# A decode step with cached attention: K turned as 32-bit words, P turned on VectorE, scores and PV in four column tiles

## The chip, the core and the metric

The kernel runs on one core of a Trainium2 chip. The metric is device time in microseconds (us), from launch to end, as the median of several runs. "Span" is the stretch that the profile covers, from the first to the last instruction of one execution; for the kernel before it is 121.3 us where the time is 123.2 us.

## What is computed

Eight tokens (B = 8, one position each) of width 512 go through layer normalisation, then through two branches: attention over a cached window, and a feed-forward net (FFN) with a gelu gate. The window W is 1024 of the 4096 cached positions; there are 32 query heads on 8 K/V heads, head width 128.

```
def reference(A_x, A_k_cache, A_v_cache, A_wq, A_wo, B_x, B_w_gate, B_w_up, B_w_down):
    xn = _layernorm(A_x)
    q = (xn @ A_wq).reshape(8, 1, 32, 128).transpose(0, 2, 1, 3)
    k = jnp.repeat(A_k_cache[:, :, 4096 - 1024:, :], 4, axis=1)
    v = jnp.repeat(A_v_cache[:, :, 4096 - 1024:, :], 4, axis=1)
    p = softmax(einsum("bhqd,bhkd->bhqk", q, k) * 128 ** -0.5)
    s = einsum("bhqk,bhkd->bhqd", p, v).transpose(0, 2, 1, 3).reshape(8, 1, 4096) @ A_wo
    g = silu((gelu(xn @ B_w_gate) * (xn @ B_w_up)) @ B_w_down)
    return A_x + s * g
```

All inputs are bf16. The K and V windows are 16 MB each, wq and wo 4 MB each, and the three FFN weights 1.75 MB each: some 47 MB that are read once.

## The kernel before

**Loads.** Every large operand goes through one ring of 20 slots of 8 KB per partition, 1 MB each (`slot`, line 73), all issued on the sync queue in program order: K of group 0, four pieces of wq, K of group 1, and then, in the main loop (line 428), V of group g and K of group g + 2, and after these the FFN weights and wo in pieces (`parts`, line 439). A piece waits for the slot that it takes to be free, and for the transfer eight places before it on the queue.

**Groups.** A group is one token and one half of the K/V heads: 4 heads of 1024 positions, 16 groups in all. The slot of a group holds in each of its 128 partitions 32 rows (`NKR`) of 128 bf16, partition 4p + n having head n. So each 128x128 block of a K slot mixes the four heads, partition by partition. Scores are computed for all 16 queries of a group (`QW`: 4 heads by 4 queries) against every key, and those of the wrong head are pushed to minus 30000 by a mask that a small matmul adds (`hot` by `far`, line 242).

**Work of a group, before.** `turn_k` (226): 32 bf16 transposes on TensorE, eight to a PSUM tile, and one VectorE copy (234) for each eight. `score` (237): the mask matmul, and 32 matmuls with a turned K block as the loaded operand and the 16 queries as the streaming one (253). Scores come out with the keys in the partitions. `soft` (264): one exponential on ScalarE (266). `values` (269): a matmul with all ones that sums P over partitions (273), 32 matmuls with a V block loaded and P streaming (282), and on VectorE a reduction of the sums (290), a reciprocal (293) and the product (294). The output of a group is already turned, as wo needs it. `regroup` (301) packs eight tokens' outputs into `og`.

**Order.** The program order on each engine is the order of the code: nothing is moved by a scheduler (`manual_schedule`). In the main loop turning and scoring of group g alternate by eights, and `values` of group g - 1 comes before the last quarter of the scores of g:

Of the kernel before, what the change touches and what calls it, by code (L numbers as in the profile page):

```python
# [8 lines left out]
ACT = mybir.ActivationFunctionType  # L9
# [7 lines left out]
def kernel(  # L17
# [13 lines left out]
    nc = tc.nc  # L31
# [28 lines left out]
    kT_pool = ctx.enter_context(tc.tile_pool(name="kT_pool", bufs=8))  # L60
    p_pool = ctx.enter_context(tc.tile_pool(name="p_pool", bufs=3))
    small = ctx.enter_context(tc.tile_pool(name="small", bufs=3))
    ffn_sb = ctx.enter_context(tc.tile_pool(name="ffn_sb", bufs=1))
    ps_t = ctx.enter_context(tc.tile_pool(name="ps_t", bufs=2, space=bass.MemoryType.PSUM))
    ps_sc = ctx.enter_context(tc.tile_pool(name="ps_sc", bufs=2, space=bass.MemoryType.PSUM))
# [39 lines left out]
    def load_down(h):  # L105
        t = slot()
        n = FR // 2 * D
        nc.sync.dma_start(
            out=t[:, 0:n],
            in_=B_w_down.rearrange("(p j) d -> p (j d)", j=FR)[:, h * n : (h + 1) * n],  # L110
        )
        return t
# [3 lines left out]
    def load_wo(h0, j0, j1):  # L116

        t = slot()
        n = (j1 - j0) // rep if j1 - j0 > rep else 1
        if n > 1:  # L120
            nc.sync.dma_start(
                out=t[:, 0 : n * rep * D].rearrange("p (h f) -> p h f", h=n),
                in_=wo_rows[:, h0 : h0 + n, :],
            )
        else:
            nc.sync.dma_start(
                out=t[:, 0 : (j1 - j0) * D],
                in_=wo_rows[:, h0, j0 * D : j1 * D],
            )
        return t  # L130
# [7 lines left out]
    for g in range(NGR):  # L138
        v_t[g] = None
    stream = []  # L140
# [13 lines left out]
    ones_pp = consts.tile([P, P], BF16, name="ones_pp")  # L154
    nc.vector.memset(ones_pp, 1.0)
# [3 lines left out]
    hot = consts.tile([HN, P], BF16, name="hot")  # L159
    nc.vector.memset(hot, 0.0)  # L160
    nc.gpsimd.affine_select(
        out=hot.rearrange("n (p m) -> n p m", m=HN),
        in_=hot.rearrange("n (p m) -> n p m", m=HN),
# [3 lines left out]
        pattern=[[0, P // HN], [-1, HN]],  # L167
        channel_multiplier=1,
    )
    far = consts.tile([HN, NKR, QW], BF16, name="far")  # L170
    nc.vector.memset(far, -30000.0)
    nc.gpsimd.affine_select(
        out=far.rearrange("n r (m j) -> n r m j", m=HN),
        in_=far.rearrange("n r (m j) -> n r m j", m=HN),
# [3 lines left out]
        pattern=[[0, NKR], [-1, HN], [0, rep]],  # L178
        channel_multiplier=1,
    )  # L180
# [19 lines left out]
    for t in range(2):  # L200
        nc.scalar.dma_start(
            out=x_res[64 * t : 64 * t + B, :], in_=x_flat[:, t * 256 : (t + 1) * 256]
        )
    xT_ps = ps_t.tile([P, 2, NDC, 32], BF16, name="t_ps")
# [13 lines left out]
    qT_all = persist.tile([P, NHALF, B, HN, rep], BF16, name="qT_all")  # L218
    oT_all = persist.tile([P, NHALF, HN, rep, B], BF16, name="oT_all")
    og = persist.tile([P, Hkv, rep, 64], BF16, name="og")  # L220
    nc.vector.memset(og, 0.0)

    kT_t = {}
    sc_t = {}

    def turn_k(g, t):
        kp = ps_t.tile([P, 8 * P], BF16, name="t_ps")
        for c in range(8):
            r = 8 * t + c
            nc.tensor.transpose(  # L230
                kp[:, c * P : (c + 1) * P], k_t[g][:, r * Dh : (r + 1) * Dh], ident
            )
        kT = kT_pool.tile([P, 8 * P], BF16, name="kT")
        nc.vector.tensor_copy(out=kT, in_=kp)  # L234
        kT_t[g, t] = kT

    def score(g, t):
        b, i = groups[g]
        if t == 0:
            sc = ps_sc.tile([P, NKR, QW], FP32, name="sc_ps")  # L240
            sc_t[g] = sc
            nc.tensor.matmul(  # L242
                sc.rearrange("p r q -> p (r q)"),
                hot,
                far.rearrange("n r q -> n (r q)"),
                start=True,
                stop=False,
                skip_group_check=True,
            )
        sc = sc_t[g]  # L250
        for c in range(8):
            r = 8 * t + c
            nc.tensor.matmul(  # L253
                sc[:, r, :],
                kT_t[g, t][:, c * P : (c + 1) * P],
                qT_all[:, i, b, :, :].rearrange("p n j -> p (n j)"),
                start=False,
                stop=True,
                skip_group_check=True,
            )  # L260

    p_t = {}

    def soft(g):
        p = p_pool.tile([P, NKR, QW], BF16, name="p")
        nc.scalar.activation(out=p, in_=sc_t[g], func=ACT.Exp, scale=inv_sqrt_dh)  # L266
        p_t[g] = p

    def values(g):
        b, i = groups[g]  # L270
        p = p_t[g]
        sums_ps = ps_a.tile([P, NKR, QW], FP32, name="a_ps")
        nc.tensor.matmul(  # L273
            sums_ps.rearrange("p r q -> p (r q)"),
            ones_pp,
            p.rearrange("p r q -> p (r q)"),
            start=True,
            stop=True,
        )
        o_ps = ps_o.tile([P, QW], FP32, name="o_ps")  # L280
        for r in range(NKR):
            nc.tensor.matmul(  # L282
                o_ps,
                v_t[g][:, r * Dh : (r + 1) * Dh],
                p[:, r, :],
                start=(r == 0),
                stop=(r == NKR - 1),
            )
        sums = small.tile([P, QW], FP32, name="sums")
        nc.vector.tensor_reduce(  # L290
            out=sums, in_=sums_ps.rearrange("p r q -> p q r"), axis=AX.X, op=ALU.add
        )
        nc.vector.reciprocal(out=sums, in_=sums)  # L293
        nc.vector.tensor_tensor(  # L294
            out=oT_all[:, i, :, :, b],
            in0=o_ps.rearrange("p (n j) -> p n j", n=HN),
            in1=sums.rearrange("p (n j) -> p n j", n=HN),
            op=ALU.mult,
        )

    def regroup(i):

        rg = ps_a.tile([P, rep, HN, B], FP32, name="a_ps")
        sel = ident.rearrange("p (e j) -> p j e", j=rep)
        for j in range(rep):
            for c in range(rep):
                nc.tensor.matmul(
                    rg[32 * c : 32 * c + 32, j, :, :],
                    sel[:, j, :],
                    oT_all[:, i, :, c, :],  # L310
                    start=True,
                    stop=True,
                    skip_group_check=True,
                    tile_position=(0, 32 * c),
                )
        nc.vector.tensor_copy(
            out=og[:, i * HN : (i + 1) * HN, :, 0:B],
            in_=rg.rearrange("p j h b -> p h j b"),
        )
# [19 lines left out]
    q_sb = persist.tile([P, NHALF, 512], BF16, name="q_sb")  # L339
    nc.vector.tensor_copy(out=q_sb[:, 0, :], in_=q_ps[0])  # L340
    nc.scalar.copy(out=q_sb[:, 1, :], in_=q_ps[1])
    for i in range(NHALF):
        qT_ps = ps_t.tile([P, rep, HN, 32], BF16, name="t_ps")
        for c in range(rep):
            nc.tensor.transpose(  # L345
                qT_ps[:, c, :, :].rearrange("p n b -> p (n b)"),
                q_sb[:, i, c * Dh : (c + 1) * Dh],
                ident,
            )
        nc.vector.tensor_copy(  # L350
            out=qT_all[:, i, :, :, :].rearrange("p b n c -> p c n b"),
            in_=qT_ps[:, :, :, 0:B],
        )
# [74 lines left out]
    for g in range(NGR + 1):  # L428
        if g < NGR:
            v_t[g] = load_kv(A_v_cache, *groups[g])  # L430
            if g + 2 < NGR:
                k_t[g + 2] = load_kv(A_k_cache, *groups[g + 2])
        if g == NGR - 1:
            wg_t = [load_up(B_w_gate, 0), load_up(B_w_gate, 1)]
            wu_t = [load_up(B_w_up, 0), load_up(B_w_up, 1)]
            wd_t = [load_down(0), load_down(1)]
        if g == NGR:

            parts = [(0, 0, 8), (2, 0, 8), (4, 0, 8), (6, 0, 4), (7, 0, 3), (7, 3, 4)]
            wo_t = [load_wo(*q) for q in parts]  # L440
        if g < NGR:
            for t in range(4):
                if g:
                    turn_k(g, t)
                    if t:
                        score(g, t - 1)
                elif t:
                    score(g, t - 1)
        if g:
            values(g - 1)  # L450
            if groups[g - 1][0] == B - 1:
                regroup(groups[g - 1][1])
        if g < NGR:
            score(g, 3)
            soft(g)

    hT = ffn_up()
    ffn_down(hT)

# [6 lines left out]
    for n, (q, at, hh, j) in enumerate(rows):  # L466
        for t in range(2):
# [3 lines left out]
                og[:, hh, j, :],  # L471
# [9 lines left out]
    nc.vector.tensor_tensor(out=out_sb, in0=tmp, in1=x_res, op=ALU.add)  # L481
# [33 lines left out]
```

After the loop come the FFN (`ffn_up` 356 and `ffn_down` 398, 32 and 28 matmuls that wait for their weights piece by piece) and the product with wo (469), 64 matmuls in two column tiles, then two VectorE operations (480, 481) and the output's two small transfers.

The softmax here doesn't subtract the row's maximum and nothing guards it: scores larger than these inputs give would overflow.

## Time and profile before

| | |
|---|---|
| time, median of 3 runs | 123.2 us (123.0 to 123.8) |
| span of the profile | 121.3 us |
| TensorE matmul busy | 96.0 us (79%), 1772 matmuls |
| TensorE weight load busy | 75.6 us (62%), 1772 loads |
| VectorE busy | 73.6 us (61%), 142 instructions |
| ScalarE busy | 14.9 us (12%), 24 instructions |
| HBM read | 47.46 MB, 391 GB/s over the span |
| a 1 MB K or V transfer, from issue to landing | 19.7 and 20.3 us (median) |
| turned K copied out of PSUM on VectorE (234) | 64 x 690 ns |
| transposes of K (230) | 512, 43.7 us busy |

The names in the rows: PE is TensorE's matmul, PEld its weight load, DVE is VectorE, ACT ScalarE, SP the sync engine that issues the large transfers, SPq its queue; L234 is line 234. A group row ends with the idle time of the engine just before these instructions, and with what ended most of it. Matmuls are pipelined, so a busy TensorE need not be one at its peak. PEclk is the clock that TensorE was granted, in tenths. In the chain of waits, each step is followed back from the end to what released it.

### The profile page before, as it was taken

The page shows a single profiled execution, that of the slowest core. Times are in us where ns is not written, and L with a number is a line of the kernel's source. Part 1 is how long each engine was busy: PE and PEld are TensorE (multiplying, and loading weights), DVE is VectorE, ACT ScalarE, POOL GpSimd, SP SyncE. Part 2 cuts the span into 40 slices and gives each one's busy share as a digit, 9 for nine tenths or more (in the row PEclk, how much of TensorE's full clock was granted, in tenths as well). Part 3 has the DMA queues.
Part 4 walks back from the last instruction along what each step waited for, and adds up shares of the span by engine and source line. Part 5 has one row for each costly group of instructions (what it writes and reads, how often), then busy time and mean ns, then how long its engine had stood idle before and what let it go on. Part 6 is the DMA issues. An engine that isn't in the chain of part 4 may idle for free.

```text
span 121.3 us, 3885 instructions
## 1 busy us (share of the span) xinstructions
PE 96.0 (79%) x1772; PEld 75.6 (62%) x1772; DVE 73.6 (61%) x142; ACT 14.9 (12%) x24; POOL 3.1 (3%) x8
## 2 busy tenths in 40 slices
PE   0197269999999999999799993999999783396660
PEld 0192028897787887887778873897888550064540
DVE  4663035475888887888688882665788644704011
ACT  4000043010101101101101101010101103002000
POOL 7200000000000000000000000000000000000000
PEclk9999955555799999999999999555799955555798
DMA  2999999999999999999999999999999999999820
GB/s 78 394 430 427 427 432 430 416 413 430 424 432 421 430 427 424 408 419 427 432 421 427 419 432 419 421 421 432 430 416 419 419 437 414 416 422 417 343 86 3
DMA packets 7392, 47.72 MB, mean 393 GB/s; under 512 B 808, under 2 KB 976, under 8 KB 2768
## 3 DMA queue, kind: packets, MB, share of 16 engines
q1 hardware_dynamic: 7312, 47.46, 93.6%
q8 instruction: 14, 0.23, 0.7%
q10 hardware_dynamic: 64, 0.02, 0.1%
q14 instruction: 2, 0.02, 0.0%
HBM read 47.46 MB, written 0.01 MB: 391 GB/s over the span
## 4 chain that ended last, share of the span: by engine, by line
DMA 56%; PE 34%; DVE 4%; SPq 2%; issue 1%; DVEq 0%
DMA slot<-in_A_k_cache_dram 17%; DMA slot<-in_B_w_up_dram 15%; PE t_ps L230 15%; DMA slot<-in_A_wo_dram 13%; DMA slot<-in_A_wq_dram 10%; PE sc_ps L253 7%; PE o_ps L282 5%; PE sc_ps L242 3%; DVE kT L234 3%; PE a_ps L273 2%; SPq L84 1%; PE t_ps L345 1%; DVE q_sb L340 1%; SPq L89 1%; PE big L469 1%
## 5 line engine op out<-in xcount | busy, mean ns | idle before, releaser
L234 DVE COPY kT<-t_ps 128x1024 bf16<-128x1024 bf16 x64 | 42.6, 690 | 17.4 <-PE t_ps L230 16.6
L230 PE MATMUL t_ps<-ident,slot 128*128 128x128 bf16 x512 | 43.7, 244 | 2.8 <-DMA slot<-in_A_k_cache_dram 2.8
L230 PEld LDWEIGHTS <-slot 128*128 128x128 bf16 x512 | 35.2, 110 | 3.3 <-DMA slot<-in_A_k_cache_dram 3.0
L253 PEld LDWEIGHTS <-kT 128*128 128x128 bf16 x512 | 18.6, 99 | 9.0 <-DVE kT L234 7.3
L253 PE MATMUL sc_ps<-qT_all,kT 128*128 128x16 bf16 x512 | 22.7, 172 | 1.8
L266 ACT ACTIVATE p<-sc_ps 128x512 bf16<-128x512 f32 x16 | 9.6, 597 | 68.1 <-PE sc_ps L253 68.1
L282 PEld LDWEIGHTS <-slot 128*128 128x128 bf16 x512 | 15.7, 98 | 3.5 <-issue 2.2
L282 PE MATMUL o_ps<-p,slot 128*128 128x16 bf16 x512 | 15.7, 171 | 0.0
L290 DVE TENSOR_REDUCE sums<-a_ps 128x16 f32<-128x512 f32 x16 | 11.1, 692 | 1.4 <-PE a_ps L273 1.0
L469 PE MATMUL big<-slot,og 128*64 128x256 bf16 x64 | 5.8, 332 | 2.8 <-DMA slot<-in_A_wo_dram 2.8
L273 PE MATMUL a_ps<-p,ones_pp 128*128 128x512 bf16 x16 | 7.1, 442 | 0.7 <-ACT p L266 0.7
L242 PE MATMUL sc_ps<-far,hot 4*128 4x512 bf16 x16 | 7.3, 453 | 0.0
L469 PEld LDWEIGHTS <-og 128*64 128x64 bf16 x64 | 4.5, 135 | 4.3 <-issue 2.8
L330 PE MATMUL big<-slot,xT 128*32 128x512 bf16 x32 | 3.4, 516 | 3.9 <-DMA slot<-in_A_wq_dram 3.9
L362 PE MATMUL big<-slot,xT 128*32 128x448 bf16 x32 | 3.6, 566 | 2.0 <-DMA slot<-in_B_w_up_dram 2.0
L294 DVE TENSOR_TENSOR oT_all<-o_ps,sums 128x16 bf16<-128x16 f32 x16 | 3.7, 230 | 1.7
L404 PE MATMUL big<-slot,hT 128*32 128x256 bf16 x28 | 3.3, 415 | 1.7 <-DVE hT L389 1.7
L330 PEld LDWEIGHTS <-xT 128*32 128x32 bf16 x32 | 0.9, 104 | 5.8 <-issue 5.7
L340 DVE CAST q_sb<-big 128x512 bf16<-128x512 f32 x1 | 0.7, 692 | 6.2 <-PE big L330 6.2
L293 DVE RECIPROCAL sums<-sums 128x16 f32<-128x16 f32 x16 | 4.0, 253 | 0.5
L480 DVE TENSOR_TENSOR tmp<-big,g_sb 128x256 f32<-128x256 f32 x1 | 0.4, 425 | 6.2 <-PE big L469 6.2
L404 PEld LDWEIGHTS <-hT 128*32 128x32 bf16 x28 | 2.1, 138 | 3.3 <-DVE hT L389 2.5
(50 smaller groups left out, 28.5 us busy)
## 6 DMA issues: line engine op xcount, KB each, us to landing
slot<-in_A_k_cache_dram SPq DMA_DIRECT2D x16, 1024.0 KB, 19.7
slot<-in_A_v_cache_dram SPq DMA_DIRECT2D x16, 1024.0 KB, 20.3
slot<-in_A_wq_dram SPq DMA_DIRECT2D x4, 1024.0 KB, 9.7
slot<-in_A_wo_dram SPq DMA_DIRECT2D x3, 1024.0 KB, 17.7
slot<-in_B_w_gate_dram SPq DMA_DIRECT2D x2, 896.0 KB, 19.4
slot<-in_B_w_up_dram SPq DMA_DIRECT2D x2, 896.0 KB, 18.6
slot<-in_B_w_down_dram SPq DMA_DIRECT2D x2, 896.0 KB
slot<-in_A_wo_dram SPq DMA_DIRECT2D x1, 512.0 KB
```

The source lines that it names most:

```text
L230: nc.tensor.transpose(kp[:, c * P : (c + 1) * P], k_t[g][:, r * Dh : (r + 1) * Dh], ident)
L234: nc.vector.tensor_copy(out=kT, in_=kp)
L242: nc.tensor.matmul(sc.rearrange("p r q -> p (r q)"), hot, far.rearrange("n r q -> n (r q)"), start=True, stop=False, skip_group_check=True,)
L253: nc.tensor.matmul(sc[:, r, :], kT_t[g, t][:, c * P : (c + 1) * P], qT_all[:, i, b, :, :].rearrange("p n j -> p (n j)"), start=False, stop ...
L266: nc.scalar.activation(out=p, in_=sc_t[g], func=ACT.Exp, scale=inv_sqrt_dh)
L273: nc.tensor.matmul(sums_ps.rearrange("p r q -> p (r q)"), ones_pp, p.rearrange("p r q -> p (r q)"), start=True, stop=True,)
L282: nc.tensor.matmul(o_ps, v_t[g][:, r * Dh : (r + 1) * Dh], p[:, r, :], start=(r == 0), stop=(r == NKR - 1),)
L290: nc.vector.tensor_reduce(out=sums, in_=sums_ps.rearrange("p r q -> p q r"), axis=AX.X, op=ALU.add)
L293: nc.vector.reciprocal(out=sums, in_=sums)
L330: nc.tensor.matmul(q_ps[i][32 * j : 32 * j + 32, :], xT[:, 0, k, :], wq_t[k][:, n0 : n0 + 512], start=(k == 0), stop=(k == NDC - 1), tile_ ...
L404: nc.tensor.matmul(f_ps[64 * t : 64 * t + 32, 0:256], hT[:, j, :], w[:, c0 : c0 + 256], start=(j == 0), stop=(j == FR - 1), tile_position= ...
L469: nc.tensor.matmul(s_ps[64 * t : 64 * t + 64, 0:256], og[:, hh, j, :], wo_t[q][:, c0 : c0 + 256], start=(n == 0), stop=(n == len(rows) - 1 ...
```

## The change

The work of a group is laid out anew.

- **K turned as 32-bit words.** Two neighbouring bf16 are taken as one fp32 word, and 128x128 words are turned at a time with an fp32 identity: 16 transposes for 32. The PSUM tile holds four of them, so there are still four copies per group; that of t = 1 goes to ScalarE. In the turned K a partition holds a pair of dimensions (even and odd), of two neighbouring rows r.
- **Scores turned round.** The queries are the loaded operand, 32 columns: 2 rows r by 16 queries, zero where the row does not fit (`q2_all`), for even and for odd dimensions. Turned K streams, 512 wide. Four column tiles of TensorE work on a quarter of the keys each: 8 matmuls for 32. The mask is one matmul of 512 as before, with the roles of its operands exchanged. The queries lie in the partitions now.
- **Sums from the exponential.** `accum_out` gives the sum over each partition.
- **P turned on VectorE**, in blocks of 32x32 (`turn_p`).
- **PV** has P as the loaded operand, 32 columns, and V streams, 256 wide, in four column tiles: 16 matmuls for 32.
- **Gather.** PV's result is copied to SBUF as fp32 on ScalarE, and three fp32 matmuls add up its pieces and the sums, turned as wo needs them.
- **Order.** A group's scores come in one piece; the turning of g + 1, the values of g - 1 and the turning of P are put between. The turned K has two buffers of a whole group in place of eight quarters; scores have one PSUM buffer in place of two, transposes three in place of two.
- **wo and the input.** wo's second and third pieces are issued as two transfers each, its last head as 2 + 1 + 1 rows in place of 3 + 1. The input for the residual is loaded on the sync queue among the pieces of wo and copied to fp32. `og` takes half the room, and the 64 columns loaded for a product with wo reach into the next entry.

The aim: fewer and longer instructions on TensorE, and less work on VectorE. The core of the diff:

```diff
-    kT_pool = ctx.enter_context(tc.tile_pool(name="kT_pool", bufs=8))
-    p_pool = ctx.enter_context(tc.tile_pool(name="p_pool", bufs=3))
+    kT_pool = ctx.enter_context(tc.tile_pool(name="kT_pool", bufs=2))
+    p_pool = ctx.enter_context(tc.tile_pool(name="p_pool", bufs=2))
+    pT_pool = ctx.enter_context(tc.tile_pool(name="pT_pool", bufs=2))
+    o_pool = ctx.enter_context(tc.tile_pool(name="o_pool", bufs=1))
-    ps_t = ctx.enter_context(tc.tile_pool(name="ps_t", bufs=2, space=bass.MemoryType.PSUM))
-    ps_sc = ctx.enter_context(tc.tile_pool(name="ps_sc", bufs=2, space=bass.MemoryType.PSUM))
+    ps_t = ctx.enter_context(tc.tile_pool(name="ps_t", bufs=3, space=bass.MemoryType.PSUM))
+    ps_sc = ctx.enter_context(tc.tile_pool(name="ps_sc", bufs=1, space=bass.MemoryType.PSUM))
...
+            step = n if h0 == 0 else 1
+            for h in range(0, n, step):
+                nc.sync.dma_start(
+                    out=t[:, h * rep * D : (h + step) * rep * D].rearrange(
+                        "p (h f) -> p h f", h=step
+                    ),
+                    in_=wo_rows[:, h0 + h : h0 + h + step, :],
+                )
...
+    def turn_k(g, t):
+        kp = ps_t.tile([P, 4 * P], FP32, name="t_ps", tag="t")
+        kw = k_t[g].bitcast(FP32)
+        for c in range(4):
+            rp = 4 * t + c
+            nc.tensor.transpose(
+                kp[:, c * P : (c + 1) * P], kw[:, rp * P : (rp + 1) * P], ident_f
+            )
+        if t == 0:
+            kT_t[g] = kT_pool.tile([P, NKR * P], BF16, name="kT")
+        copy = nc.scalar.copy if t == 1 else nc.vector.tensor_copy
+        copy(out=kT_t[g][:, t * 8 * P : (t + 1) * 8 * P], in_=kp.bitcast(BF16))
...
+        kT = kT_t[g].rearrange("w (r k e) -> w r k e", k=P, e=2)
+        nc.tensor.matmul(
+            sc,
+            hot.rearrange("n r q -> n (r q)"),
+            far,
...
+        for e in range(2):
+            for t in range(4):
+                nc.tensor.matmul(
+                    sc[32 * t : 32 * t + 32, :],
+                    q2_all[:, i, b, e, :, :, :].rearrange("w r n j -> w (r n j)"),
+                    kT[:, :, 32 * t : 32 * t + 32, e],
+                    start=False,
+                    stop=(e == 1),
+                    skip_group_check=True,
+                    tile_position=(0, 32 * t),
+                )
...
+        nc.scalar.activation(
+            out=p, in_=sc_t[g], func=ACT.Exp, scale=inv_sqrt_dh, accum_out=acc
+        )
...
+        nc.vector.transpose(out=pT, in_=p)
+        nc.vector.tensor_scalar(
+            out=ss, in0=selq, scalar1=acc[:, 0:1], scalar2=None, op0=ALU.mult
+        )
...
+        for m in range(NKR // 2):
+            u = m % 4
             nc.tensor.matmul(
+                o_ps[32 * u : 32 * u + 32, :],
+                pT_t[g][:, m * 32 : (m + 1) * 32],
+                v_t[g][:, m * 256 : (m + 1) * 256],
...
+        nc.scalar.copy(out=o_sb, in_=o_ps)
...
+            a_ps[:, 0, :], ones_f, ss_t[g], start=True, stop=True, skip_group_check=True
+        for r in range(2):
             nc.tensor.matmul(
+                a_ps[:, 1, :],
+                o_t[g][:, r * Dh : (r + 1) * Dh],
+                selr[:, r, :],
...
-            parts = [(0, 0, 8), (2, 0, 8), (4, 0, 8), (6, 0, 4), (7, 0, 3), (7, 3, 4)]
-            wo_t = [load_wo(*q) for q in parts]
+            parts = [(0, 0, 8), (2, 0, 8), (4, 0, 8), (6, 0, 4), (7, 0, 2), (7, 2, 3), (7, 3, 4)]
+            wo_t = [load_wo(*q) for q in parts[:3]]
+            for t in range(2):
+                nc.sync.dma_start(
+                    out=x_res[64 * t : 64 * t + B, :], in_=x_flat[:, t * 256 : (t + 1) * 256]
+                )
+            wo_t += [load_wo(*q) for q in parts[3:]]
         if g < NGR:
-            for t in range(4):
-                if g:
-                    turn_k(g, t)
-                    if t:
-                        score(g, t - 1)
-                elif t:
-                    score(g, t - 1)
+            score(g)
+            soft(g)
+        if g + 1 < NGR:
+            turn_k(g + 1, 0)
+        if g < NGR:
+            turn_p(g)
+        if g + 1 < NGR:
+            turn_k(g + 1, 1)
         if g:
             values(g - 1)
+        if g + 1 < NGR:
+            turn_k(g + 1, 2)
+            turn_k(g + 1, 3)
+        if g:
+            gather(g - 1)
             if groups[g - 1][0] == B - 1:
                 regroup(groups[g - 1][1])
-        if g < NGR:
-            score(g, 3)
-            soft(g)
+    x_f = persist.tile([P, D // 2], FP32, name="x_f")
     hT = ffn_up()
     ffn_down(hT)
+    nc.vector.tensor_copy(out=x_f, in_=x_res)
```

## The prediction

> **What bounds the kernel now.** I read the page's slices and DMA queues first, then the transfer queue's own waits, then windows at the end, then the chain of waits. Slices and queues (a digit is a tenth of a slice of 3.03 us):
>
> ```profile
> PEclk9999955555799999999999999555799955555798
> DMA  2999999999999999999999999999999999999820
> ...
> q1 hardware_dynamic: 7312, 47.46, 93.6%
> q8 instruction: 14, 0.23, 0.7%
> ```
>
> The 16 DMA engines are full from the second slice to the 38th: 47.46 MB through one queue. TensorE (79% busy) and VectorE (61%) look heavy too, so the question is whether they ever hold a transfer up. Waits of the transfer queue (us in total, times, longest):
>
> ```profile
> SPq L89 <- DMA slot<-in_A_k_cache_dram: 27.2, 13, 3.4
> ...
> SPq L89 <- PE t_ps L230: 1.8, 5, 0.6
> ```
>
> A transfer is issued when the one eight before it has landed. TensorE's freeing of a slot ends such a wait last only a dozen times in all, 4 us together and never more than 0.6 us, while a transfer lands some 20 us after issue, so that delay never starves the engines. Ten-microsecond windows, columns PE, PEld, DVE, ACT, POOL busy, clock, DMA share, GB/s:
>
> ```profile
> 20.00:30.00 10.00, 10.00 (x143) 8.46 (x142) 5.86 (x10) 0.98 (x2) 0.00 (x0) 0.50 1.00 420
> ...
> 40.00:50.00 10.00, 9.68 (x239) 8.20 (x236) 8.52 (x16) 1.19 (x2) 0.00 (x0) 1.00 1.01 421
> ```
>
> TensorE halves its clock and the DMA rate does not notice: 420 against 421 GB/s. So two things alone set the end: 47.46 MB, unchanged by the edit, and how evenly the 16 engines finish. Half-microsecond windows:
>
> ```profile
> 113.50:114.00 0.50, 0.50 (x9) 0.36 (x6) 0.00 (x0) 0.00 (x0) 0.00 (x0) 0.94 1.05 416
> 114.00:114.50 0.50, 0.05 (x2) 0.00 (x0) 0.00 (x0) 0.00 (x0) 0.00 (x0) 1.00 0.72 285
> ...
> 115.50:116.00 0.50, 0.50 (x10) 0.33 (x7) 0.00 (x0) 0.00 (x0) 0.00 (x0) 1.00 0.35 137
> ...
> 117.00:117.50 0.50, 0.31 (x6) 0.31 (x7) 0.00 (x0) 0.00 (x0) 0.00 (x0) 1.00 0.03 10
> ```
>
> From 114.0 to 117.4 us only half to a third of the engines still work. The trace keeps the 16 completions of each transfer; their lags behind the first one say why:
>
> ```
> transfer done at   lags of its 16 parts (us)
>  20.64             all within 0.4
>  24.42             one at 1.7, the others within 0.4
>  71.09             seven at 1.5-1.7
>  75.06             one at 3.3, seven at 1.5-1.7
> 117.45 (the last)  five at 2.9-3.1, three at 1.4-1.7, eight within 0.8
> ```
>
> Each step is one packet of the queue "instruction": 16 KB, about 0.94 us, at 22.3, 29.3, 37.4, ... 73.0, ... 100.6, 116.2 us. Each sets one engine back by about 1.3 us for good; the first eight go to eight different engines, and the ninth (73.0 us) comes to the first one again. The last bytes wait for an engine hit twice. The chain ends
>
> ```profile
> 101.12 16.03 DMA slot<-in_A_wo_dram
> 117.15 0.04 issue
> 117.19 0.64 PE big L469 x8
> ```
>
> and then 0.9 us of VectorE and the output.
>
> **What the Trainium skill says.** "Runtime: NRT & Kernel Launch", section Instruction fetch mechanics: an engine's instructions come in 16 KiB blocks of 256, by a DMA queue of their own; it calls the cost "mostly hidden". The trace agrees on size (14 packets for 3,544 TensorE instructions), not on the cost, which shows as the lag above. "TensorE: Matmul & The Clock Gate", Terms: on trn2 the transpose mode is 4x faster for FP32, so one pass; Part 4 there: transposes do not count as activity for the clock. No run here shows an fp32 transpose; on the second, this trace has full clock from 31.6 to 76.0 us with transposes in every group. "TensorEngine Tiling (Array Packing)", Key Properties: a change of tiling mode drains TensorE; the edit adds four such changes per group, and no row of the trace isolates one.
>
> **The change part by part.** A group is 1 MB of K and 1 MB of V: 2 x 2.44 us = 4.88 us of DMA. The groups that carry it now:
>
> ```profile
> L234 DVE COPY kT<-t_ps 128x1024 bf16<-128x1024 bf16 x64 | 42.6, 690 | 17.4 <-PE t_ps L230 16.6
> L230 PE MATMUL t_ps<-ident,slot 128*128 128x128 bf16 x512 | 43.7, 244 | 2.8 <-DMA slot<-in_A_k_cache_dram 2.8
> ```
>
> In the chain a group takes 4.44 us at full clock (L273 at 35.32 and 39.76) and 6.19 us at half (24.45 to 30.64).
>
> *TensorE per group.* K: 16 fp32 transposes for 32. Eight of the old ones take 0.48 us at full clock, 0.87 at half, so one is 57 to 109 ns. The new one compiles to one load and one matmul. Low: the same 57/109 ns. High: load and stream not overlapped, twice that. I take the low end: 0.9/1.7 us. Mask: 0.32/0.54 as now (L242). Scores: 8 matmuls of N=512 in four tiles; L330 has that form, 0.61/1.04 us. PV: 16 of N=256 in four tiles; from L469 (16 in two tiles 1.06) and L404 (28 in two tiles 3.29 at half clock): 0.53/0.94. Gather: three fp32 matmuls, compiled as two passes each, six at some 0.1: 0.6. Four drains: nothing at the low end, the 170 ns of a small matmul (L253: 172) each at the high end; I take 0.3. Sum 3.3/5.1 us; high end (transposes doubled, drains 0.7) 4.6/7.2. Gone: 32+32 small matmuls and the 128x512 sum (L273).
>
> *VectorE per group.* Now 4 x 0.69 + 0.69 (L290) + 0.25 + 0.23 = 3.9. After: 3 x 0.69, reciprocal 0.25, product 0.23, a scale of 16 elements some 0.2, and the turn of P, 128x512: L389 turns 128x448 in 0.98 us, "VectorE: DVE Perf Modes" (The three transpose paths) gives 311 ns for 128x128, so 0.7 to 1.1; I take 0.9. Sum 3.65. *ScalarE*: exp 0.6 and its accumulator, one K copy of 1024 (twice L341's 0.58: 1.1), o_sb 0.4: about 2.2, from 0.6.
>
> *New waits.* kT has two buffers of a whole group, sc_ps one. So a loop closes: scores (0.6), pipe end (0.2), exp (0.7), turn of P (0.9) and scale (0.2) on VectorE, behind which the K copies t=2 and t=3 queue (1.4), and these release the next scores; with hops 0.3: 4.3 us at full clock, about 5.0 at half. Behind scores stand all of the next turn and values. 4.3 is under 4.88, 5.0 just over. values(g-1) also comes to stand behind K(g+1), which lands directly after V(g-1): 2.4 us later than needed, hidden by the 20-slot ring except in the last group, where no K follows. So attention stays paced by DMA: last V lands 94.6, its end near 98, as now (98.8). The FFN then waits for its weights as now (last w_up at 103.2). **Worth nothing**, hidden under the stream; the limit is attention's end at about 102 us, because 3.4 (L362 at half clock) + 1.6 (L386, L389) + 3.3 (L404) + 7.7 (64 of L469 at half clock) must fit before the last 3.4 us (VectorE 0.9, output 2.5).
>
> *What reaches the end: fewer instructions.* Compiled, TensorE has 964 loads and 964 matmuls, from 1,772 each. That is 1,928 / 256 = 7.5 blocks for 13.8, so 7 or 8 fetches instead of 14, and none of the eight engines is hit twice. The last lag falls from 3.1 to 1.7: **minus 1.4 us**. All else at the end: pieces of 2+1+1 KB for 3+1 KB per partition (packets 46 ns per 1 KB, 121 per 3 KB, eight per engine) and five more transfers with their completion packets (9 ns): +0.15. The last piece still carries two matmuls, and only two others may queue before it instead of six: -0.1 at full clock, +0.1 if TensorE is at half clock then. x_res goes behind wo's third tile, sixteen 512 B packets: under +0.1; its copy to fp32 ends before the last piece. Start-up constants lie under the first K (5.85 us). Sum -1.3: span 120.0, time 121.9.
>
> **Rivals.** *No gain, 123.1.* The fetches might not spread as I read them (more of them, or the same engine again), or the finer pieces and the x_res transfers cost what the lag gives back. For: the 1.4 us rests on a count of blocks. Against: the eight-step pattern is plain. Time 123.2 - 1.4 + 1.3. *TensorE bound, slower, 126.* For: the clock is at half for about 47 of 121 us already, and a less dense stream may keep it so. Then 5.1 per group gives 18 + 17 x 5.1 = 105 us for attention (18 is where the first scores start now), + 3.4 + 1.6 + 3.3 + 7.7 + 3.4 = 124 span, 126 with the 1.9 us that time has over span. With the high end, 18 + 17 x 7.2 = 140, about 162. Against: at half clock the stream would be dense, and the dense stream here did bring the clock back (at 31.6 and 86.3). *More gain, 120.8:* the lag goes to 0.4, if fetches fall where an engine waits anyway; nothing speaks for it, the engines never wait.
>
> **How the numbers follow.** Forecast 0.62; of its spread (121.2 to 122.6) about three quarters lies below 122.0, the 1% line. No gain 0.20. Slower 0.14. More gain 0.04. So faster 0.51, same 0.35, slower 0.14. Range: below, 121.0 (the forecast less its doubtful tenths, plus half of "more gain"); above, 123.9, which takes in "no gain" and the first tenths of a TensorE bound.
>
> **What would show it.** Right: queue "instruction" with 7 or 8 packets; DMA share full to about 114 and gone by 116; K's transposes 100 to 250 ns each, TensorE under 70% busy; the DMA queue's waits still ended by DMA. Wrong: transfers late because a slot was freed late, w_up or wo waiting for TensorE rather than the reverse, half clock throughout, a last spread still near 3 us.

## The result: 121.5 us, and where the 1.6 us went

The changed kernel takes 121.49 us (median of four runs, 121.38 to 121.84) against 123.12 us for the kernel before. The ratio is 0.986, with a 95% interval of 0.982 to 0.990: 1.4% faster, clear of the noise though small. Forecast were 121.9 us in a range of 121.0 to 123.9.

Slices and queues of the page after:

```profile
PEclk9999555569599999999999999999999755559997
DMA  2999999999999999999999999999999999999940
...
q1 hardware_dynamic: 7520, 47.46, 94.7%
q8 instruction: 7, 0.11, 0.3%
```

The DMA engines are full from the second slice to the 38th, as before, and move the same 47.46 MB. The queue "instruction" has 7 packets where it had 14. The transfer queue's own waits (us in total, times, longest):

```profile
SPq L91 <- DMA slot<-in_A_k_cache_dram: 24.0, 13, 3.1
...
SPq L91 <- PE t_ps L247: 2.2, 6, 0.5
```

The balance has not moved: transfers wait for transfers, and TensorE's freeing of a slot ends such a wait six times on this line, for at most half a microsecond. Ten-microsecond windows (columns PE, PEld, DVE, ACT, POOL busy, clock, DMA share, GB/s):

```profile
20.00:30.00 10.00, 7.17 (x42) 4.73 (x41) 5.42 (x10) 6.19 (x10) 0.00 (x0) 0.67 1.02 427
...
40.00:50.00 10.00, 9.90 (x120) 7.62 (x108) 7.76 (x19) 4.99 (x10) 0.00 (x0) 1.00 1.00 419
```

Again the DMA rate does not care about TensorE's clock. What changed is the end. Half-microsecond windows there, same columns:

```profile
115.00:115.50 0.50, 0.48 (x8) 0.43 (x8) 0.00 (x0) 0.00 (x0) 0.00 (x0) 1.00 0.48 170
115.50:116.00 0.50, 0.50 (x10) 0.25 (x6) 0.00 (x0) 0.00 (x0) 0.00 (x0) 1.00 0.22 74
116.00:116.50 0.50, 0.46 (x6) 0.18 (x3) 0.00 (x0) 0.00 (x0) 0.00 (x0) 1.00 0.00 0
```

Before, a third of the engines were still at work in 115.5 to 116.0 and some until 117.4; now the share is 0.22 there and nothing is left after 116.3. The lags of the last transfer's sixteen parts, from the trace's completions:

```
         last landing  lags of its 16 parts behind the first (us)
before   117.45        eight within 0.8, three at 1.4-1.7, five at 2.9-3.1
after    116.26        nine within 0.9, seven at 1.5-1.9
```

Seven fetches of instructions, seven parts late by one step, none by two. The trace does not name the engine that carries a fetch; that each fetch sets back one engine, and that they go round eight, is read from such counts, and the table further down tests it. The first engines end near 114.4 in both kernels; only the last ones end earlier. The chain of waits after ends

```profile
106.30 8.68 DMA slot<-in_A_wo_dram
...
115.02 1.25 PE big L535 x14
...
116.31 0.32 PE big L535 x2
```

followed by VectorE's 0.44 and 0.43 us and the output. From last landing to VectorE's first operation it is 0.38 us, before it was 0.40. So of the span's 1.5 us (121.3 to 119.8), 1.2 are the earlier landing, and some 0.2 lie behind VectorE's last operation, in the output and the closing (2.5 us before, 2.3 after).

In 89 runs of the kernel before beside these experiments the times form two clusters, 122.8 to 123.3 us (48 runs, median 123.03) and 123.5 to 124.1 us (41 runs, median 123.79), so that a median of such a kernel depends on how many runs fall into each.

### The profile page after: what moved, and what is told of

It is laid out like the page before. It is cut to its first block, busy times and chain, and to the rows that moved or that the text cites. A ratio compares the mean times of both kernels' runs of the same rounds, so it can differ in the third digit from the quotient of the medians.

```text
span 119.8 us, 2368 instructions
## 1 busy us (share of the span) xinstructions
PE 90.7 (76%) x964; PEld 63.7 (53%) x964; DVE 65.3 (54%) x149; ACT 40.3 (34%) x77; POOL 3.8 (3%) x9
## 3 DMA queue, kind: packets, MB, share of 16 engines
q1 hardware_dynamic: 7520, 47.46, 94.7%
HBM read 47.46 MB, written 0.01 MB: 396 GB/s over the span
## 4 chain that ended last, share of the span: by engine, by line
DMA 49%; PE 30%; DVE 13%; ACT 2%; SPq 2%; issue 2%; DVEq 0%
DMA slot<-in_A_k_cache_dram 16%; PE t_ps L247 16%; DMA slot<-in_B_w_down_dram 15%; DMA slot<-in_A_wq_dram 11%; DVE kT L253 10%; DMA slot<-in_A_wo_dram 7%; PE sc_ps L273 6%; PE o_ps L307 4%; SPq L86 1%; PE big L535 1%; ACT q_all L404 1%; DVE q_all L404 1%; PE t_ps L396 1%; DVE q_sb L388 1%; ACT p L286 1%
## 5 line engine op out<-in xcount | busy, mean ns | idle before, releaser
L253 DVE COPY kT<-t_ps 128x1024 bf16<-128x1024 bf16 x48 | 31.8, 688 | 21.2 <-PE t_ps L247 19.2
L247 PE MATMUL t_ps<-ident_f,slot 128*128 128x128 f32 x256 | 38.6, 302 | 3.3 <-DMA slot<-in_A_k_cache_dram 3.2
L247 PEld LDWEIGHTS t_ps<-ident_f,slot 128*128 128x128 f32 x256 | 31.3, 154 | 13.2 <-issue 7.4
L253 ACT COPY kT<-t_ps 128x1024 bf16<-128x1024 bf16 x16 | 16.2, 1012 | 12.1 <-PE t_ps L247 11.7
L273 PE MATMUL sc_ps<-kT,q_all 128*32 128x512 bf16 x128 | 10.5, 397 | 3.4 <-DVE kT L253 1.7
L294 DVE STREAM_TRANSPOSE pT<-p 128x512 bf16<-128x512 bf16 x16 | 11.2, 703 | 2.7 <-ACT p L286 2.7
L307 PE MATMUL o_ps<-slot,pT 128*32 128x256 bf16 x256 | 10.8, 292 | 0.0
L327 PE MATMUL a_ps<-selr,o_sb 128*128 128x16 f32 x64 | 10.0, 270 | 0.3 <-ACT o_sb L317 0.3
L327 PEld LDWEIGHTS a_ps<-selr,o_sb 128*128 128x128 f32 x64 | 8.8, 200 | 0.5 <-ACT o_sb L317 0.4
L317 ACT COPY o_sb<-o_ps 128x256 f32<-128x256 f32 x16 | 6.0, 376 | 1.8 <-PE o_ps L307 1.8
L388 DVE CAST q_sb<-big 128x512 bf16<-128x512 f32 x2 | 1.3, 686 | 6.5 <-PE big L375 6.5
```

The costliest lines, as they stand in the source:

```text
L247: nc.tensor.transpose(kp[:, c * P : (c + 1) * P], kw[:, rp * P : (rp + 1) * P], ident_f)
L253: copy(out=kT_t[g][:, t * 8 * P : (t + 1) * 8 * P], in_=kp.bitcast(BF16))
L273: nc.tensor.matmul(sc[32 * t : 32 * t + 32, :], q2_all[:, i, b, e, :, :, :].rearrange("w r n j -> w (r n j)"), kT[:, :, 32 * t : 32 * t + ...
L294: nc.vector.transpose(out=pT, in_=p)
L307: nc.tensor.matmul(o_ps[32 * u : 32 * u + 32, :], pT_t[g][:, m * 32 : (m + 1) * 32], v_t[g][:, m * 256 : (m + 1) * 256], start=(m < 4), st ...
L317: nc.scalar.copy(out=o_sb, in_=o_ps)
```

## The experiments

**The theories.** 1: the last landing is set by the engine that instruction fetches hit most often; 7 or 8 fetches make it early, 9 or more late. 2: the finer pieces of wo and the moved x_res gave the gain. 3: less work on TensorE gave it. 4, which the trace of after suggested: the closing sequence looks at the completion semaphores in a fixed order (0.06 us apart in the trace), and three more transfers in all (nine pieces of wo for six) moved the outputs three places on, to the last of them.

**Part of the change alone: the end.** The end's edits put into the kernel before (b_tail), and taken out of the one after (a_oldtail).

```diff
-            parts = [(0, 0, 8), (2, 0, 8), (4, 0, 8), (6, 0, 4), (7, 0, 3), (7, 3, 4)]
-            wo_t = [load_wo(*q) for q in parts]
+            parts = [(0, 0, 8), (2, 0, 8), (4, 0, 8), (6, 0, 4), (7, 0, 2), (7, 2, 3), (7, 3, 4)]
+            wo_t = [load_wo(*q) for q in parts[:3]]
...
+            wo_t += [load_wo(*q) for q in parts[3:]]
...
+    nc.vector.tensor_copy(out=x_f, in_=x_res)
```

> The kernel before with only the end changed as in the kernel after: wo's pieces cut finer, the residual input loaded on the sync queue among them and copied to fp32; attention as before, so 14 instruction blocks are fetched. Theory 1 (the gain comes from fewer fetches of TensorE instructions, none of the DMA engines being set back twice): 123.1 us, no gain, within 0.3. Theory 2 (the finer end gave the gain): about 121.5 us. Theory 3 (the lighter load of TensorE and VectorE gave it): 123.1 us.

> The kernel after with the end as it was before: wo in six pieces, the residual input loaded early on the ScalarE queue and not copied. Attention stays new, 7 fetches. Theory 1: 121.5 us, within 0.3. Theory 2: about 123 us. Theory 3: 121.5 us.

b_tail: 122.89 us (122.60 to 123.56) beside 123.16, ratio 0.997 [0.995, 0.999]. It has 14 fetches, five engines at 2.8 to 3.0, and its last landing is at 117.58. a_oldtail: 121.84 us (121.49 to 122.32), ratio 0.987 [0.983, 0.991], with 7 fetches and a last landing at 116.11. So the end's edits alone give about 0.3 of the 1.6 us (with whatever the closing order gives, as both runs move the outputs' place too), and without them most of the gain is there: theory 2 falls as the main cause. But a_oldtail's chain has an end of its own:

```profile
95.51 18.04 DMA slot<-in_A_wo_dram
...
113.59 3.60 PE big L528 x32
```

Its windows say why (columns as above):

```profile
113.00:114.00 1.00, 0.45 (x6) 0.41 (x6) 0.00 (x0) 0.00 (x0) 0.00 (x0) 0.50 1.01 406
114.00:115.00 1.00, 1.00 (x13) 1.00 (x10) 0.00 (x0) 0.00 (x0) 0.00 (x0) 0.50 0.67 262
115.00:116.00 1.00, 1.00 (x14) 1.00 (x12) 0.00 (x0) 0.00 (x0) 0.00 (x0) 0.50 0.27 97
```

A whole megabyte of wo landed at 113.55 and put 16 products into line at once, with TensorE at half clock; these and the 16 that came after take until 117.2, a microsecond past the last landing. With finer pieces the first eight of these 16 need not wait for the second half of their megabyte.

**Cutting PV in two: 9 fetches instead of 7.** Same work for DMA, VectorE and ScalarE, same end, 512 more instructions on TensorE.

```diff
-            nc.tensor.matmul(
-                o_ps[32 * u : 32 * u + 32, :],
+            for h in range(2):
+                nc.tensor.matmul(
+                    o_ps[32 * u : 32 * u + 32, 128 * h : 128 * h + 128],
...
-                v_t[g][:, m * 256 : (m + 1) * 256],
+                    v_t[g][:, m * 256 + 128 * h : m * 256 + 128 * h + 128],
```

> The kernel after with each PV matmul of N=256 cut into two of N=128: 512 more TensorE instructions, 9.6 blocks for 7.6, so 9 fetches, the ninth on an engine that was set back already; last spread near 3 us instead of 1.9. TensorE gets about 1 us more to do per group and stays below the DMA time of a group. Theory 1: 122.6 us (plus 1.0 to 1.4). Theory 2: 121.5. Theory 3: 121.5 to 122, as TensorE is 76% busy now and would be some 85%.

122.73 us (122.54 to 122.91), ratio 0.994 [0.992, 0.997]: three quarters of the gain are gone (1.24 of 1.63 us), though TensorE is busy for 88.5 us, no more than the 90.7 us of after. Page and windows:

```profile
PE 88.5 (73%) x1220; PEld 63.9 (53%) x1220; DVE 65.2 (54%) x149; ACT 40.2 (33%) x77; POOL 3.8 (3%) x9
...
q8 instruction: 9, 0.15, 0.4%
```

```profile
115.50:116.00 0.50, 0.00 (x0) 0.00 (x0) 0.00 (x0) 0.00 (x0) 0.00 (x0) 1.00 0.22 76
116.00:116.50 0.50, 0.48 (x8) 0.43 (x8) 0.00 (x0) 0.00 (x0) 0.00 (x0) 1.00 0.07 25
116.50:117.00 0.50, 0.49 (x10) 0.23 (x6) 0.00 (x0) 0.00 (x0) 0.00 (x0) 1.00 0.06 20
```

From 116.0 to 117.3 a share of 0.06 to 0.07 is one engine of sixteen. Its lag is 2.9 us, and all the others are within 1.8. The ninth fetch, at 100.3 us, came to an engine that had been hit before, and this one engine holds the end back by 1.0 us.

**Cutting the scores in two: 8 fetches.** The control for the last one: 256 more instructions, one more block.

```diff
-                nc.tensor.matmul(
-                    sc[32 * t : 32 * t + 32, :],
+                for h in range(2):
+                    nc.tensor.matmul(
+                        sc[32 * t : 32 * t + 32, 256 * h : 256 * h + 256],
...
-                    kT[:, :, 32 * t : 32 * t + 32, e],
+                        kT[:, 8 * h : 8 * h + 8, 32 * t : 32 * t + 32, e],
```

> The kernel after with each score matmul of N=512 cut into two of N=256: 256 more TensorE instructions, 8.6 blocks for 7.6, so 8 fetches, and still no engine set back twice. Theory 1: 121.5 us, no change, last spread 1.9 us; with the run of nine fetches it makes a step and not a slope. Theory 2: 121.5. Theory 3: between the kernel after and the run with twice as many added instructions.

121.49 us (121.38 to 121.53), ratio 0.984 [0.980, 0.987], 8 fetches, last spread 1.9, last landing 116.24. The eighth fetch costs nothing, the ninth 1.2 us (a_pv2 less this run). It is a step, not a slope.

**The kernel before with fewer instructions.** b_pv4 leaves out 28 of a group's 32 PV products, b_few leaves out 24 of 32 score products and 24 of 32 PV products. First the edit of b_pv4, then that of b_few:

```diff
-        for r in range(NKR):
+        for r in (0, 10, 20, 31):
```

```diff
-        for c in range(8):
+        for c in (0, 4):
...
-        for r in range(NKR):
+        for r in (0, 5, 10, 15, 20, 25, 30, 31):
```

> The kernel before with 4 of the 32 PV matmuls of a group kept and 28 left out (the sum over the other V rows is missing). TensorE and its loads get 0.7 us per group shorter; 10.4 instruction blocks for 13.9, so 10 fetches, two engines still set back twice. Theory 1 (fetches set the end): 123.1 us, no gain, last spread near 3 us. Theory 3 (TensorE's load): a part of the gain, 122.3 to 122.8 us.

> The kernel before with 8 of 32 score matmuls and 8 of 32 PV matmuls of a group kept, the others left out (most scores are the mask alone, most V rows are missing). 7.9 blocks, so 7 or 8 fetches, no engine set back twice; the end with wo as before. Theory 1: 121.7 us (minus 1.3 to 1.5), last spread 1.7 us. Theory 2 (the finer end gave the gain): 123.1. Theory 3: about 121.5.

b_pv4: 122.97 us (122.66 to 123.84) beside 123.55, ratio 0.998 [0.996, 1.000]; the two medians lie in different clusters, so the ratio, not their difference, is what counts (the means are 123.17 and 123.43). TensorE lost a quarter of its instructions and the time barely moved: theory 3 falls. It has 10 fetches, and two engines at 3.1. b_few: 122.14 us (121.65 to 122.49), ratio 0.990 [0.986, 0.993]; 8 fetches, last spread 1.7, last landing 116.05. This is the kernel before in everything else, bf16 transposes and VectorE's copies included, and its last landing is where that of after is. Like a_oldtail it has the coarse pieces, and its profiled run ends with 32 products with wo in 3.64 us at half clock. That run took 122.46 us; the two fastest took 121.65 and 121.70, close to after. So the coarse end fits most of the 0.65 us that the median lacks against after.

**No attention, and nothing but transfers.** a_one replaces the attention of after by one small product per K or V slot. a_zero also touches wq's and the FFN's slots only, and uses the first and last row of each piece of wo.

```diff
-            score(g)
-            soft(g)
...
-            turn_k(g + 1, 1)
+            touch(k_t[g + 1])
         if g:
-            values(g - 1)
...
-            gather(g - 1)
+            touch(v_t[g - 1])
```

> The kernel after with attention left out: each K and V slot is only read by one small matmul, the attention output is zero; projections, FFN and wo stay. TensorE almost idle until the FFN, 1.9 blocks, so one or two fetches instead of seven. Theory 1: one engine set back once is enough to hold the end, so no more than 0.3 us under the kernel after: 121.2 to 121.5 us. Theory 3: well below it, 120 us or less.

> The transfers alone: each slot is read by one or a few small matmuls, all else of the computation is left out, the output is the input rounded through. 0.6 blocks, so no fetch at all. Theory 1: the last spread is the 0.5 us of the start and the time 1.2 to 1.4 us below the kernel after, 120.2 us. Theory 3: the same as the run without attention.

a_one: 121.42 us (121.21 to 121.45), ratio 0.984 [0.981, 0.986]. TensorE fell from 76% to 22% of the span, at full clock throughout, and the time by 0.07 us:

```profile
PE 26.2 (22%) x244; PEld 13.4 (11%) x244; DVE 15.2 (13%) x38; ACT 8.6 (7%) x13; POOL 3.8 (3%) x9
...
q8 instruction: 2, 0.03, 0.1%
```

One engine is 1.7 us behind, the others are within 0.8. Of the two fetches only the one at 61.3 us can be behind this: the other came at 114.3 us, when the parts of the last transfer had begun to land. So theory 3, which gave 120 us or less, falls again. a_zero: 120.48 us (120.37 to 121.07), ratio 0.977 [0.974, 0.979]; there is no line "instruction" on its page, all parts are within 0.7, and the last landing is at 115.05. The step from a_zero to a_one is 0.94 us in time and 0.95 us in the last landing, so it is not the smaller work at the end of a_zero. One early fetch costs as much as seven.

**The order of the closing sequence.** Three tiny loads of x in the kernel before, so that its outputs come to the last of the completion semaphores (b_lane3), and five in the kernel after, which brings its outputs back to the place that they had before (a_lane5).

```diff
+    spare = persist.tile([B, 32 * 3], BF16, name="spare")
+    for t in range(3):
+        nc.scalar.dma_start(
+            out=spare[:, 32 * t : 32 * t + 32], in_=x_flat[:, 32 * t : 32 * t + 32]
+        )
```

> The kernel before with three tiny unused loads (8x32 of x) on the ScalarE queue after the normalisation. They move the two output transfers by three places in the eight completion semaphores that transfers take in turn, to the two that the closing sequence waits for last. Theory 4 (0.2 us of the kernel after's gain is that its output transfers hold the last two semaphores, so that no further waits follow them): 122.9 us, minus 0.2, and the time from the last landing to the end of the span goes from 1.0 to 0.8 us. Without it: 123.15 us.

> The kernel after with five tiny unused loads (8x32 of x) on the ScalarE queue, which move its output transfers to the semaphores that they have in the kernel before, with waits for three others behind them. Theory 4: 121.7 us, plus 0.2. Without it: 121.5 us.

In the profiled runs the stretch from the outputs' landing to the end of the span is 1.0 us in before and in a_lane5, 0.8 in after and in b_lane3, as theory 4 has it. The times: b_lane3 123.38 us beside 123.19, ratio 0.999 [0.997, 1.001]; but 12 of its 22 runs fell into an upper cluster. Taken apart, its lower cluster (122.65 to 122.88) lies below the lower one of before (median 123.03), and the upper (123.35 to 123.66) below the upper (123.79), each by some 0.2. a_lane5 is 121.56 us, only 0.07 more than after. So this is worth 0.2 us at most, and the times alone do not settle it.

**The pieces of wo by themselves.** After, with the six old pieces, but x_res where the change puts it; three tiny loads keep the outputs' place.

```diff
-            parts = [(0, 0, 8), (2, 0, 8), (4, 0, 8), (6, 0, 4), (7, 0, 2), (7, 2, 3), (7, 3, 4)]
+            parts = [(0, 0, 8), (2, 0, 8), (4, 0, 8), (6, 0, 4), (7, 0, 3), (7, 3, 4)]
```

> The kernel after with wo in the six pieces of before, the residual input still on the sync queue, and three tiny unused loads so that the output transfers keep the last two semaphores. If the finer pieces matter because TensorE has 32 products of wo to do after a 1 MB piece lands 2.5 us before the end (3.6 us at half clock, 2.1 at full): 121.5 us where the clock is full in that stretch and 122 where it is half, so 121.7 in the median. If they do not matter: 121.5 us.

121.77 us, ratio 0.986 [0.982, 0.990]: three runs at 121.25 to 121.48 and three at 122.06 to 122.07. The coarse pieces bring the two clusters back, 0.7 us apart; with finer pieces (after, a_sc2, a_pv2) there is one, and among b_tail's 22 runs all but one are within 122.6 to 123.2. The three upper runs have mean clocks of 0.835 to 0.858, the lower ones 0.883 to 0.896. The profiled run was a lower one, and the clock came back in time:

```profile
113.00:114.00 1.00, 0.31 (x6) 0.31 (x7) 0.21 (x1) 0.00 (x0) 0.00 (x0) 1.00 1.02 411
114.00:115.00 1.00, 0.82 (x16) 0.63 (x14) 0.09 (x1) 0.00 (x0) 0.00 (x0) 1.00 0.63 245
```

Compare a_oldtail's windows above: 0.50 there, and TensorE busy without a gap.

Finer pieces do not do away with the half clock. Of a_lane5's six runs five took 121.38 to 121.64 us and one 122.00, and that one was profiled:

```profile
106.20 8.67 DMA slot<-in_A_wo_dram
...
114.92 1.93 PE big L540 x16
```

```profile
115.00:116.00 1.00, 1.00 (x12) 1.00 (x13) 0.00 (x0) 0.00 (x0) 0.00 (x0) 0.50 0.30 103
```

The last landing is at 116.17 us, as in after, but at half clock the last 16 products run until 116.85, where those of after end at 116.6. So with finer pieces half clock at the end cost about half a microsecond in this run, with coarse ones some 0.7.

**Once more the kernel before**, for a profile of an upper run.

> The kernel before, unchanged, for one more trace of it. Its single runs fall into two clusters, 122.8 to 123.3 us and 123.5 to 124.1 us. Theory: in the upper cluster TensorE is at half clock when the coarse pieces of wo land, and the products with wo outlast the last landing. So if this run falls into the upper cluster (about 45 in 100): granted clock 0.5 from about 112 us on, a chain that ends with some 32 products with wo in about 3.6 us from 114 us, last landing near 117.4 as ever, span about 122.0. If it falls into the lower one: clock near 1.0 at the end, a chain that ends with the eight products after the last landing, span about 121.3, and nothing new. Rival: an upper run with full clock at the end, or with a last landing some 0.7 us later: then the clusters come from the transfers and not from TensorE.

It was a lower run, 123.12 us, and so tells nothing new: clock 0.72 in 113 to 114, 1.00 after, and the chain of before. That the upper cluster of the kernel before is the half clock at the end is thus argued from a_oldtail, b_few, a_lane5 and a_pieces; no profile shows it in that kernel itself. Its mean clocks do not show it either: they overlap, 0.813 to 0.888 in the lower cluster and 0.803 to 0.860 in the upper.

The fetches, side by side (times are medians; "coarse" or "fine" are the pieces of wo):

| kernel | fetches | engines near 3 us behind | last landing | time |
|---|---|---|---|---|
| a_zero, fine | 0 | none | 115.05 | 120.48 |
| a_one, fine | 2 | none (one at 1.7) | 116.00 | 121.42 |
| after, fine | 7 | none | 116.26 | 121.49 |
| a_sc2, fine | 8 | none | 116.24 | 121.49 |
| b_few, coarse | 8 | none | 116.05 | 122.14 |
| a_pv2, fine | 9 | one | 117.29 | 122.73 |
| b_pv4, coarse | 10 | two | 117.40 | 122.97 |
| b_tail, fine | 14 | five | 117.58 | 122.89 |
| before, coarse | 14 | five | 117.45 | 123.12 |

Nine fetches, one engine hit twice; ten, two. Fourteen give five and not six, because the last of them comes at 116.2 us in before (116.0 in b_tail), too late to hold anything up, as does the eighth of b_few, at 114.7. With these left out, every row has as many engines near 3 us behind as it has fetches beyond eight. The last landing has three levels, near 115, 116 and 117.4 us, for no hit, one and two.

## Why the prediction was right, and where its sums were off

**What bounds the kernel: right.** The stream of 47.46 MB and the spread of its engines. a_one shows how far this goes: with most of TensorE's work gone, the time is the same. One line of the prediction's table of lags was misread: at 71.09 us eight parts, not seven, are 1.5 to 1.7 us late, one for each of the eight fetches until then, which speaks for its mechanism.

**The term that was to bring the gain: right, and of the size given.** Forecast were 7 or 8 fetches for 14 and minus 1.4 us. The pair with equal (fine) ends, b_tail and after, differs by 122.89 - 121.49 = 1.40 us, and a_pv2 less after is 1.24. "The Trainium skill", page "Runtime: NRT & Kernel Launch", section Instruction fetch mechanics, calls the cost of a block "mostly hidden". In this kernel, which waits for all sixteen DMA engines, it is not, and the measurement decides: the first fetch on any engine costs about a microsecond (a_zero to a_one, 0.94 us) and the second on one engine 1.2 to 1.4.

**The end's edits, costed at about nothing: mis-sized.** The steps were +0.15 for smaller pieces, under +0.1 for x_res, and -0.1 or +0.1 for the products queued before the last piece, "at full clock" or "at half clock". The runs show about -0.3: b_tail is 0.27 under before, a_oldtail 0.35 over after, and a_pieces, which keeps the outputs' place in the closing order and x_res where the change puts it, 0.28 over after. The sign of the half-clock case was wrong. The step counted what queues before the very last piece; what matters at half clock is the line that forms when a whole megabyte lands at once, with 32 products behind it in 3.6 us (a_oldtail). If the upper cluster of before is this, nearly half of its runs pay 0.6 to 0.8 us for it, and the profile of before, a lower run, could not show it. With this term the forecast would have been 123.2 - 1.4 - 0.3 = 121.5.

**TensorE: the loop's time near by luck, its path and the load wrong.** Groups of after, as the page has them:

```profile
L253 DVE COPY kT<-t_ps 128x1024 bf16<-128x1024 bf16 x48 | 31.8, 688 | 21.2 <-PE t_ps L247 19.2
L247 PE MATMUL t_ps<-ident_f,slot 128*128 128x128 f32 x256 | 38.6, 302 | 3.3 <-DMA slot<-in_A_k_cache_dram 3.2
...
L253 ACT COPY kT<-t_ps 128x1024 bf16<-128x1024 bf16 x16 | 16.2, 1012 | 12.1 <-PE t_ps L247 11.7
...
L294 DVE STREAM_TRANSPOSE pT<-p 128x512 bf16<-128x512 bf16 x16 | 11.2, 703 | 2.7 <-ACT p L286 2.7
```

The chain of waits through one group:

```profile
36.73 1.30 DVE kT L253 x2
...
38.08 0.62 PE sc_ps L273 x8
38.70 1.02 PE t_ps L247 x8
39.72 0.55 PE o_ps L307 x16
40.27 0.60 PE t_ps L247 x4
```

A group takes 4.16 us at full clock (the next copies are at 40.89), against 4.3 forecast and the stream's 4.88. That the two are so close is luck: the loop does not run by way of the exponential and the turn of P, as the prediction had it; it runs through TensorE's own line, which stands ready behind the scores, and only the last two copies are waited for. Eight fp32 transposes take 1.02 us, so one is some 128 ns: above the low end of 57 that was taken, and somewhat above the high end, twice that. "TensorE: Matmul & The Clock Gate", Terms, calls the transpose mode 4x faster for fp32 on trn2; the trace puts the price of one at about twice that of a bf16 transpose (60 ns in before). So sixteen are 2.05 us for the 0.9 taken. Two of the signs named for a right prediction failed with it: TensorE is 76% busy, not under 70, and the row above has a mean of 302 ns for a transpose, not 100 to 250. The other terms were near: scores 0.55 to 0.62 us for 0.61, PV 0.55 for 0.53, the gather 0.13 + 0.45 in the chain at 33.10 for 0.6. No row isolates the four drains. With the mask's 0.32 the terms make about 4.1 us for the 3.3 forecast, nearly the whole 4.16. TensorE was thus nearer to being the bound than forecast: in 40 to 50 us it is busy for 9.90 of 10 us.

**VectorE and ScalarE: right.** 3 x 0.69 + 0.70 + 0.19 + 0.25 + 0.23 = 3.4 us for the 3.65 forecast; the turn of P took 0.70, the low end of its bounds, and less than four times the 311 ns that "VectorE: DVE Perf Modes", The three transpose paths, gives for a 128x128 block (1.24 us by proportion, an estimate from that page). ScalarE: 0.60 + 0.19 for the accumulator's read + 1.01 + 0.38 = 2.2, as forecast.

**Missed, without effect: the start.** The queries' copies run in turn:

```profile
19.11 0.73 DVE q_all L404
...
19.86 0.73 ACT q_all L404
...
20.62 0.74 DVE q_all L404
```

Eight such, four of q_sb (L388) and, behind ScalarE's last one, a table load of 1.28 us put the first exponential at 25.5 us where it was at 19.8. The prediction took the start as unchanged. The ring hides it: the loop gains 4.88 - 4.16 = 0.7 us per group, and is back at the pace of the stream at 68.8 us, where the chain has a transfer again. Attention ends at 98.2 us; forecast was near 98, before it was 99.1.

**Rivals.** "No gain" falls with the table of fetches, though a_pv2 shows how near it was: two blocks more, and it would have been the result. "TensorE bound" did not come about: the clock was at half only for most of 12 to 33 us and from 94 to 108, and full in the loop between. At full clock a group takes 4.16 us of the stream's 4.88; what it would take at half clock throughout, no run shows. Its "for", that a thinner stream may keep the clock low, stays open: a_one, with TensorE busy for 22%, never left full clock, so it shows only that a thin stream alone does not bring the half clock.

## What to carry to other kernels

When all DMA engines are full to the end, ask not only how many bytes there are but which engine ends last, and look at the completions of the last transfer part by part. Instructions are traffic too: count the blocks of the longest instruction stream, and expect a step where the count passes the number of engines that they go round (eight here), not a saving in proportion. And cut the last megabytes so that no long line of products forms behind one landing: the clock may not be there when it is needed.

## What the runs showed that was not expected

- **One early fetch costs as much as eight.** The last landing goes 115.05, 116.0 to 116.3, and 117.3 to 117.6 us, for 0, 2 to 8 (of the 2 only one was early enough to count), and 9 to 14 fetches. A level is set by one engine alone.
- **Nearly half the runs of a kernel can be 0.7 us slower, most likely for want of clock in its last 4 us.** Before: 48 of 89 runs at 122.8 to 123.3, 41 at 123.5 to 124.1; a_pieces: three and three. That the pieces of wo make the two clusters is shown by a_pieces and b_tail; the clock is shown in profiles of other kernels only. Finer pieces leave one cluster, with a rare run above it.
- **Closing order.** The stretch from the outputs' landing to the end of the span is 1.0 or 0.8 us, by the place of the outputs' semaphores (three places moved it to 0.8, five more brought it back). In the times it is not settled.
- **fp32 transposes of 128x128 at about 128 ns** in a stream at full clock, twice a bf16 one, so that per byte they are no cheaper; what they halve is the number of instructions.
